# Forming the first expert block from batches 0 to 2 and routing all tokens between its products

## The chip, the cores and the metric

One Trainium2 chip, one core. The metric is the device time of one execution in microseconds (us): the median of the runs of the kernel before is 931.78 us (3 runs, 931.18 to 934.29). Engines by the names of the profile: PE is TensorE (matmuls; PEld is its weight load), DVE is VectorE, ACT is ScalarE, POOL is GpSimd (here it issues the indirect DMAs), SP is SyncE (here it issues the other DMAs).

## What is computed

Three stages in float32, one after the other on 1792 tokens (4 batches of 448) of width 768.

1. Attention, 12 heads of 64: `sigmoid(q k^T / 8 - log 448) v` for each batch. Its output is the token matrix x.
2. A mixture of 8 experts. A token takes part if `x . w_skip > 0`; it goes to the expert e with the largest of 8 logits `x @ w_gate`, and gets `x + gate * relu(x @ w1[e]) @ w2[e]`, where gate is the softmax probability of that expert (w1[e] is 768 x 1024, w2[e] 1024 x 768). Other tokens pass unchanged.
3. A dense layer pair, 768 to 2048 to 768, with an ELU between.

For the inputs of the reference (its default seed), worked out from the reference itself: 1066 tokens take part. Per expert 0 to 7 they are 0, 65, 199, 144, 391, 35, 10 and 222; of the first 1280 tokens the same counts are 0, 1, 128, 0, 298, 35, 9 and 83.

## The kernel before

Products of full precision are made of three matmuls of rounded parts: `gemm` (line 724) adds hi x hi, hi x lo and lo x hi. So each operand is split into a hi part (ACT, a copy that rounds) and a lo part (DVE, `tensor_sub`).

**Attention.** The loop at line 434 goes over n = 0 to 24. Step n computes the scores of head pair n (`scores`, line 223, PE, then a sigmoid on ACT) and the mix of pair n - 1 (`mix`, line 239, PE, then a copy to xT on DVE). Pairs 18 to 23 are batch 3. Between these the loop places, by hand, other work: the splits of the next q and k; the logits of a finished batch (`logits`, line 252, and `token_logits`, line 277); `rows(t)` (line 266), which transposes one tile of 128 tokens of xT and writes it to x_d in DRAM, for tiles 0 to 8 (`LATE = 9`); `narrow` (line 143), which converts 18 of the dense layer's weight tiles on DVE, spread evenly over the 24 pairs; and `sooner` (line 389), which picks experts for the first 10 tiles (`SOON`, 1280 tokens) and counts their places.

**Routing.** After the loop everything about the last batch is done in a row (lines 493 to 637): its logits, rows 9 to 13, the choice of experts, the counts by expert, the order of blocks, the place of each token in its block (`inv`, line 585: a product of one-hot matrices whose result is the list of tokens of every block), the gates (`ig`, line 622) and the kind of every block. PE is kept busy meanwhile with products of zeros (`keep_warm`, line 191, 28 of them) and, ahead of the first block, `hold_up` (line 739, 14 products).

**Expert blocks.** A block is up to 256 tokens of one expert, as two halves of 128. Blocks are sorted so that those with the fullest last block come first. `level(i, k)` (line 1088) handles block i: `gather` (line 696, two indirect DMAs on POOL) brings its rows of x_d into xg; `fetch` (line 684, SP) brings the expert's eight weight chunks of 768 KB into a ring of raw tiles; `split_w` (line 710) splits a chunk; `columns` (line 755) transposes xg on PE and splits it into x2; then four chunks of the product with w1 (`up_two`, line 806), and four with w2 for each half (`back`, line 857); `outcome` (line 905) adds the gated result to xg and `scatter` writes it back. Of the second product of a block three chunks of its first half are left to the next block (`between`, line 953, and `lead_in`, line 967), so that PE has work while the next x2 is split. The kind of a block, a number read into a register, decides by branches whether its second half is left out (1), takes at most 64 tokens (2) or is whole (3). In the first block 0, aside from its products, `places_in_order` (line 974) and `slot_order` (line 1029) work out an order of all tokens by expert for the dense stage.

All three of PE, ACT and DVE follow the order in which the program is written (`manual_schedule`); each engine takes its instructions strictly in that order.

Of the kernel before, what the change touches and what calls it, by code (L numbers as in the profile page):

```python
# [32 lines left out]
E = 8  # L33
# [5 lines left out]
NB = (NT + E * (BLK - 1)) // BLK  # L39
# [7 lines left out]
LATE = 9  # L47
NRAW = 13
NSPL = 4
# [5 lines left out]
SOON_STEP = (B - 1) * NP + 1  # L55
NEG = -(2**31)
# [8 lines left out]
def _constants():  # L65
# [8 lines left out]
        "row": np.arange(P)[:, None],  # L74
# [15 lines left out]
def build(nc, tc, a):  # L90
# [3 lines left out]
    with ExitStack() as top:  # L94
# [35 lines left out]
        blk_e = cp.tile([P, 1], I32, name="blk_e")  # L130

        early = top.enter_context(tc.tile_pool(name="early", bufs=1))
        raw_t = [early.tile([P, WCH], F32, name=f"raw{j}") for j in range(2)]
        wi1 = early.tile([P, DM], F32, name="wi1")
# [36 lines left out]
        ET = mybir.EngineType  # L171
        with ExitStack() as st:
            st.enter_context(tc.manual_schedule(engines={ET.PE, ET.Activation, ET.DVE}))
            xp = st.enter_context(tc.tile_pool(name="xp", bufs=1))
            rowp = st.enter_context(tc.tile_pool(name="rowp", bufs=2))
            ast = st.enter_context(ExitStack())
            qkp = ast.enter_context(tc.tile_pool(name="qkp", bufs=2))
            atp = ast.enter_context(tc.tile_pool(name="atp", bufs=2))
            cvp = ast.enter_context(tc.tile_pool(name="cvp", bufs=2))
            pss = st.enter_context(tc.tile_pool(name="pss", bufs=3, space=PSUM))  # L180
            ps1 = st.enter_context(tc.tile_pool(name="ps1", bufs=1, space=PSUM))
            psx = st.enter_context(tc.tile_pool(name="psx", bufs=1, space=PSUM))
# [18 lines left out]
            lgT = xp.tile([P, NT], F32, name="lgT")  # L201
# [50 lines left out]
            def logits(b):  # L252
                lg = psx.tile([P, 512], F32, name="lg", tag="px")
                for cc in range(KD):
# [9 lines left out]
                nc.vector.tensor_copy(lgT[:, b * S : (b + 1) * S], lg[:, :S])  # L264

            def rows(t):
                xr = rowp.tile([P, DM], F32, name="xr")
                px = pss.tile([P, 2, 512], F32, name="px", tag="ps")
                for i in range(KD):
                    g, o = i // 3, i % 3 * P  # L270
                    flip(px[:, g, o : o + P], xT[:, i, t * P : (t + 1) * P])
                nc.scalar.copy(xr.rearrange("p (g n) -> p g n", g=2), px[:, :, :N2])
# [4 lines left out]
            def token_logits(t0, n):  # L277
                pl = psx.tile([P, 4, P], F32, name="pl", tag="px")
                for i in range(n):
                    flip(pl[:, i, :], lgT[:, (t0 + i) * P : (t0 + i + 1) * P])  # L280
# [25 lines left out]
            per = [ert([1, E1], f"per{j}", BF16) for j in range(2)]  # L306
            t1 = ert([NTT, E1], "t1")
            pos_i = ert([NTT], "pos_i", I32)
            sr_i = ert([NTT, 1], "sr_i", I32)
            rt_tok = ert([NTT, P], "rt_tok", F16)  # L310

            def choices(a, z):
# [22 lines left out]
                yield  # L335
                with nc.allow_low_precision("whole numbers up to 14"):
                    nc.vector.reduce_sum(
                        per[a > 0][:, 0], oh1[:, w].rearrange("p t e -> p e t"), axis=AX.X
                    )

# [3 lines left out]
            def positions(a, z, pool, tag):  # L344

                pos = pool.tile([P, z - a, E1], F32, name="pos", tag=tag)
                n, w = z - a, oh1[:, a:z]
                if a:
                    nc.tensor.matmul(
                        pos, ones_b, per[0].to_broadcast([P, n, E1]), start=True, stop=False  # L350
                    )
                else:
                    nc.tensor.matmul(pos, zero_b[:, 0], w, start=True, stop=False)
                for o in range(1, n):
                    nc.tensor.matmul(
                        pos[:, o:, :],
                        ones_b,
                        w[:, o - 1 : o].to_broadcast([P, n - o, E1]),
                        start=False,
                        stop=False,  # L360
                        skip_group_check=True,
                    )
                nc.tensor.matmul(pos, tri_b, w, start=False, stop=True)
                return pos

            def places(a, z, pos):
# [6 lines left out]
                nc.vector.tensor_copy(pos_i[:, w], posv[:, w])  # L373
                yield
                nc.vector.tensor_scalar(sr_i[:, w, 0], pos_i[:, w], P - 1, None, op0=ALU.bitwise_and)
# [3 lines left out]

            def spots(a, z):  # L380

# [7 lines left out]
            def sooner():  # L389

                yield from choices(0, SOON)
                for _ in range(NCH):
                    yield
                pos = positions(0, SOON, psx, "px")
                yield from places(0, SOON, pos)
                yield from spots(0, SOON)
# [5 lines left out]
            def load_v(n):  # L402
                vts[n] = qkp.tile([CP, 4, NCH, D], F32, name="vt", bufs=2)
# [16 lines left out]
            zrow = rowp.tile([1, DM], F32, name="zrow", bufs=1)  # L420
            nc.gpsimd.memset(zrow, 0.0)
            nc.sync.dma_start(x_d[NT : NT + 1, :], zrow)

# [10 lines left out]
            for n in range(steps + 1):  # L434
                b, hp = divmod(n, NP)
                T, p = divmod(n, 2)
                if p == 0 and n < steps:
# [16 lines left out]
                if conv is None and narrowed < n * 2 * FA // (steps - 1):  # L454
# [898 lines left out]
```

## Time and profile before

| | |
|---|---|
| median of 3 runs | 931.78 us |
| the profiled execution's own time | 926.99 us |
| its span, first to last instruction | 925.2 us |
| mean granted TensorE clock | 0.995 |
| PE busy | 894.3 us, 97% |
| DVE busy | 556.0 us, 60% |
| ACT busy | 485.6 us, 52% |
| POOL busy | 72.3 us, 8% |
| stages | attention to 167.8 us, routing to 190.8, experts to 449.2, dense to 925.2 |

The busy time of PE counts its products of zeros too. A table of 40 slices shows PE at 8 or 9 tenths everywhere, so the places where time goes are seen only in the rows of single instructions. The profiled execution is 4.8 us shorter than the median of the runs; sums below are made against the profiled execution and carried over to the median as a difference.

### The profile page before, as it was taken

The numbers are of one execution on the slowest core, as the hardware profiler recorded it, in microseconds if no ns is written. First come the engines' busy times: TensorE is split into PE (matmuls) and PEld (weight loads), VectorE is DVE, ScalarE is ACT, GpSimd is POOL, SyncE is SP. The second block draws the span as 40 slices with busy tenths as digits, with TensorE's granted clock in tenths as the row PEclk, the third lists the DMA queues.
The fourth block names the chain that finished last, engine by engine and source line by source line (L and its number), as shares of the span: only waits on it lengthen the run. The fifth ranks groups of instructions, "written<-read, shape, count | busy, mean of one in ns | idle before, by whom it ended". The sixth has DMA issues, their size and how long they took to land.

```text
span 925.2 us, 13707 instructions
## 1 busy us (share of the span) xinstructions
PE 894.3 (97%) x5239; PEld 719.4 (78%) x5239; DVE 556.0 (60%) x862; ACT 485.6 (52%) x676; POOL 72.3 (8%) x69
## 2 busy tenths in 40 slices
PE   9999999898999998799899999999999999999998
PEld 4445555488988997688688888888888888888997
DVE  2776677766664654787588887534434533434664
ACT  7767767343454454676354554444443444443664
POOL 0000000203010310232100000100000100000100
PEclk9999999999999999999999999999999999999999
DMA  8778785599552961982653342100100100000100
GB/s 285 239 250 269 243 299 170 182 381 413 188 215 68 365 237 40 410 322 85 222 194 103 103 119 69 65 5 0 35 18 18 69 1 1 1 1 4 66 1 35
DMA packets 33909, 133.95 MB, mean 145 GB/s; under 512 B 4666, under 2 KB 5818, under 8 KB 33810
## 3 DMA queue, kind: packets, MB, share of 16 engines
q1 hardware_dynamic: 29186, 113.43, 34.7%
q0 software_dynamic: 4480, 19.01, 5.8%
q8 instruction: 57, 0.93, 0.4%
q14 instruction: 42, 0.34, 0.1%
q10 hardware_dynamic: 144, 0.23, 0.1%
HBM read 112.08 MB, written 23.60 MB: 147 GB/s over the span
## 4 chain that ended last, share of the span: by engine, by line
PE 94%; DVE 2%; issue 1%; ACT 1%; DMA 1%; POOL 0%; ACTq 0%; DVEq 0%; POOLq 0%
PE acc L1228 16%; PE pt L1228 10%; PE acc L1195 8%; PE acc L1196 8%; PE acc L1197 8%; PE po L242 8%; PE ps L228 7%; PE acc L725 6%; PE acc L726 6%; PE acc L727 6%; PE pt L138 1%; PE acc L797 1%; PE acc L138 1%; PE acc L798 1%; PE px L138 1%
## 5 line engine op out<-in xcount | busy, mean ns | idle before, releaser
L718 DVE TENSOR_TENSOR wlo<-raw,whi 128x1536 fp32r<-128x1536 f32 x64 | 111.3, 1755 | 36.6 <-ACT whi L716 32.6
L1204 ACT ACTIVATE m<-acc 128x512 f32<-128x512 f32 (+1 forms) x64 | 34.9, 545 | 174.0 <-PE acc L1197 167.1
L1206 DVE SCALAR_TENSOR_TENSOR m<-m,acc 128x512 f32<-128x512 f32 (+1 forms) x64 | 39.7, 620 | 137.6 <-ACT m L1205 137.6
L716 ACT CAST whi<-raw 128x1536 fp32r<-128x1536 f32 x64 | 94.0, 1481 | 29.9 <-PE acc L727 9.0
L235 ACT ACTIVATE at<-ps,bias 112x896 f32<-112x896 f32 x96 | 88.9, 1009 | 28.3 <-PE ps L228 27.9
L1228 PE MATMUL acc<-wol,gh 128*128 128x256 f32 x320 | 101.0, 316 | 0.0
L1228 PE MATMUL acc<-woh,gl 128*128 128x256 f32 x320 | 100.5, 314 | 0.0
L1228 PE MATMUL acc<-woh,gh 128*128 128x256 f32 x320 | 100.4, 314 | 0.0
L1196 PE MATMUL acc<-x,wih 128*128 128x512 f32 (+1 forms) x270 | 96.0, 356 | 0.0
L1195 PE MATMUL acc<-x,wih 128*128 128x512 f32 (+1 forms) x270 | 95.9, 355 | 0.0
L1197 PE MATMUL acc<-x,wil 128*128 128x512 f32 (+1 forms) x270 | 95.6, 354 | 0.0
L725 PE MATMUL acc<-whi,both 128*128 128x384 f32 (+1 forms) x236 | 84.4, 357 | 3.4 <-issue 3.4
L726 PE MATMUL acc<-wlo,both 128*128 128x384 f32 (+1 forms) x236 | 83.1, 352 | 0.0
L727 PE MATMUL acc<-whi,both 128*128 128x384 f32 (+1 forms) x236 | 83.1, 352 | 0.0
L242 PE MATMUL po<-at,vt 112*64 112x448 f32 x384 | 77.5, 545 | 0.7 <-DVE xT L250 0.7
L1184 DVE TENSOR_TENSOR wol<-wo,woh 128x768 fp32r<-128x768 f32 x64 | 61.2, 956 | 23.4 <-ACT woh L1183 23.0
L1228 PEld LDWEIGHTS acc<-woh,gh 128*128 128x128 f32 x320 | 60.3, 188 | 10.1
L1228 PEld LDWEIGHTS acc<-wol,gh 128*128 128x128 f32 x320 | 60.3, 188 | 9.3
L1183 ACT CAST woh<-wo 128x768 fp32r<-128x768 f32 x64 | 53.4, 834 | 26.0 <-PE acc L1228 25.9
L1210 DVE TENSOR_TENSOR gl<-m,gh 128x512 fp32r<-128x512 f32 (+1 forms) x64 | 40.0, 625 | 40.5 <-ACT gh L1209 40.5
L1178 DVE TENSOR_TENSOR wil<-wi,wih 128x768 fp32r<-128x768 f32 x60 | 57.4, 956 | 11.0 <-ACT wih L1177 6.0
L1228 PEld LDWEIGHTS acc<-woh,gl 128*128 128x128 f32 x320 | 60.1, 188 | 4.3
(235 smaller groups left out, 1881.5 us busy)
## 6 DMA issues: line engine op xcount, KB each, us to landing
raw<-in_w SPq DMA_DIRECT2D x66, 768.0 KB
raw<-in_wi SPq DMA_DIRECT2D x9, 768.0 KB
raw<-in_wo SPq DMA_DIRECT2D x9, 768.0 KB
vt<-in_v SPq DMA_DIRECT2D x12, 448.0 KB
x_d<-xr SPq DMA_DIRECT2D x14, 384.0 KB
raw<-in_wi SPq DMA_DIRECT2D x14, 384.0 KB
raw<-in_wo SPq DMA_DIRECT2D x14, 384.0 KB
qr<-in_q SPq DMA_DIRECT2D x11, 448.0 KB
```

The costliest lines, as they stand in the source:

```text
L228: nc.tensor.matmul(ps[:CP, j, :S], kk[head, p, c * CP : (c + 1) * CP], qq[head, p], start=(i == 0), stop=(i == 2),)
L235: nc.scalar.activation(at[:, :, c, :], ps[:CP, :, :S], AF.Sigmoid, bias=bias[:CP], scale=QK_SCALE)
L242: nc.tensor.matmul(po[64 * j : 64 * j + 64, :S], vt[:, 2 * (hp % 2) + j, c, :], at[:, j, c, :], start=(c == 0), stop=(c == NCH - 1),)
L716: nc.scalar.copy(w_hi, raw)
L718: nc.vector.tensor_sub(w_lo, raw, w_hi)
L725: nc.tensor.matmul(o, a_hi, b_hi, start=first, stop=False)
L726: nc.tensor.matmul(o, a_hi, b_lo, start=False, stop=False)
L727: nc.tensor.matmul(o, a_lo, b_hi, start=False, stop=last)
L1195: nc.tensor.matmul(o, a, b, start=(cc == 0), stop=False)
L1196: nc.tensor.matmul(o, a, c, start=False, stop=False)
L1197: nc.tensor.matmul(o, wil[:, cc], b, start=False, stop=(cc == KD - 1))
L1228: nc.tensor.matmul(o, a, b, start=(clears and f == 0 and k_ == 0), stop=(f == KF2 - 1 and k_ == 2), skip_group_check=True,)
```

## The change

1. **A first block from 1280 tokens.** `sooner` starts one step earlier. It now takes the expert with the most tokens among batches 0 to 2, takes its first 256 tokens (`took`), and with ten small products (`inv0`) makes the list of their rows, `slot_0`, in step 23. `gather_first` brings them into xg. Its weights are fetched by the expert's number `blk_0`: chunks 0 and 1 at step 23, 2 and 3 at step 24 into tiles that lie where q and k lay, 4 and 5 behind them, 6 and 7 once the raw tiles of 0 and 1 are split.
2. **The first products follow the attention.** `columns(0)` comes right after the last mix. `first_block` computes the block without branches; its 256 places are all computed.
3. **The routing goes between its products.** `routing()` is a generator with a step behind each of the 16 groups of nine products with w1, and four behind each chunk with w2: the last batch's token logits, rows 10 to 13, counts (less `took`), places, lists, gates, kinds, then `places_in_order`. All `keep_warm` calls behind the attention and `hold_up` are gone. The remaining tokens make blocks 1 and up (`NB` is one larger, `RING`-tile lgT, slots count from block 1).
4. **What moves into the attention.** `rows(9)` (`LATE = 10`; rows 7 to 9 at steps 19 to 21), the 18 conversions (now done by step 21 instead of 23, and all of them written to DRAM, so that wi1 is read back), the first four of six products of the last batch's logits (ahead of the last mix).
5. **Pools.** The x2 tile, xT and the attention's tiles move to the other side of SBUF, so that the weight tiles can take q's and k's place early; `rows_of` in the dense stage reuses two xg tiles.

How the instructions move, at the three places that the prediction speaks of. First PE, from the end of the attention on. Before (po is the mix, lg the logits, px rows, pl the token logits):

```order
L242 MATMUL po<-at,vt 64x448 x16
L256 MATMUL lg<-xT,wgs 32x448 x6
L138 MATMUL px<-cst,xT 128x128 x6
L138 MATMUL pl<-cst,lgT 128x128 x4
L138 MATMUL px<-cst,xT 128x128 x12
```

And in the change, from the last of the ten products of inv0 (pc are the first transposes of the gathered rows; twelve of them follow, then two more logit products of L271, then the first expert product, L548):

```order
L479 MATMUL inv_1797<-a_192,rt_tok 128x2
L256 MATMUL po<-at,vt 64x448 x8
L271 MATMUL lg<-xT,wgs 32x448 x4
L256 MATMUL po<-at,vt 64x448 x8
L142 MATMUL pc<-cst,xg_108 128x128
L142 MATMUL pc<-cst,xg_109 128x128
```

The last two mixes are now parted by four logit products, and twelve transposes of gathered rows and the other two logit products are all that stands between the last mix and the first expert product. Second DVE, inside the first block: the choice of experts for the last batch ends, then two splits of weights stand among the routing's instructions.

```order
L373 TENSOR_TENSOR oh<-sc,m_175 128x4x8
L541 TENSOR_TENSOR wlo_1835<-raw_107,whi_1834 128x1536
L745 SCALAR_TENSOR_TENSOR ni<-acc_1908,took 128x8
L748 TENSOR_SCALAR nb<-ni 128x8
L751 TENSOR_SCALAR last<-ni 128x8
L752 SCALAR_TENSOR_TENSOR rank<-last,early_cst 128x8
L756 TENSOR_TENSOR first<-rank 128x64
L759 TENSOR_TENSOR tmp<-nb,first 128x64
L760 TENSOR_REDUCE span<-tmp 128x8
L541 TENSOR_TENSOR wlo_1913<-raw_1836,whi_1912 128x1536
```

Before, the routing's instructions stood ahead of all splits but that of chunk 0; now the splits of chunks 1 to 7 and the copies of the block stand between them. Third POOL: the two gathers of the first block (xg_108 and xg_109, by slot_0) come ahead of the last batch's choice of experts (oh 128x4), which before came ahead of every gather.

```order
L524 DMA xg_108<-x_d,slot_102 128x768
L524 DMA xg_109<-x_d,slot_102 128x768
L356 TENSOR_SCALAR oh<-lgt 128x4
L771 TENSOR_TENSOR posk<-posv,skip 128x4
L513 DMA xg_1918<-x_d,slot_tok 128x768
L513 DMA xg_1919<-x_d,slot_tok 128x768
```

The gathers of block 1 (xg_1918 and xg_1919) wait for the lists of all blocks, slot_tok.

The core of the diff:

```diff
-LATE = 9
+LATE = 10
+NRAW0 = 6
...
             def sooner():
 
...
+                bank = psx.tile([P, 512], F32, name="pos", tag="px")
+                pos, count = positions(0, SOON, bank)
+                yield
+                nc.vector.scalar_tensor_tensor(
+                    key, count, float(E), con("ramp")[:, :E], op0=ALU.mult, op1=ALU.add
+                )
+                yield
+                nc.vector.reduce_max(kmax, key, axis=AX.X)
...
+                nc.vector.scalar_tensor_tensor(
+                    took[:, 0], count, float(BLK), sel, op0=ALU.min, op1=ALU.mult
+                )
...
+                yield from wait(SOON_STEP + 4, 0)
+                inv = psx.tile([P, 512], F32, name="inv0", tag="px")[:, :2]
+                for t in range(SOON):
+                    nc.tensor.matmul(
+                        inv, rt_tok[:, t, :], a0[:, t, :], start=(t == 0), stop=(t == SOON - 1)
+                    )
+                yield
+                nc.vector.tensor_scalar_add(slot_0, inv, float(NT))
+                gather_first()
...
+                if n == steps - 1:
+                    assert narrowed == 2 * FA
+                    fetch(0, range(2))
+                if n == steps:
+                    qst.close()
...
+                    some_weights(tokp, 2, 2)
+                    fetch(0, range(2, 4))
+                    lg = logits(B - 1, None, range(KD - 2))
...
-                if conv is None and narrowed < n * 2 * FA // (steps - 1):
+                if conv is None and narrowed < min(2 * FA, n * 2 * FA // (steps - 3)):
...
             run(soon)
-            logits(B - 1)
+            columns(0, [pss.tile([P, 2, 512], F32, name="pc", tag="ps")[:, 0] for _ in range(3)])
+            logits(B - 1, lg, range(KD - 2, KD))
...
+            def routing():
...
+                token_logits(done_lgt, NTT - done_lgt, acc_t[5])
+                yield
+                choose(SOON, NTT)
+                split_w(0, 1, hi=False)
+                fetch(0, range(NRAW0, 8))
+                rows(LATE, banks)
+                yield
+                rows(LATE + 1, banks)
+                pos, cnt = positions(SOON, NTT, acc_t[5])
...
+                inv = acc_t[4][:, :NHB]
+                for t in range(NTT):
+                    nc.tensor.matmul(
+                        inv, rt_tok[:, t, :], aa[:, t, :], start=(t == 0), stop=(t == NTT - 1)
+                    )
+                nc.vector.tensor_scalar_add(slot_tok, inv, float(NT))
+                gather(1, False)
...
+                coming = kind(1)
...
+                fetch(1, range(2))
+                yield from places_in_order()
+                yield
+                order_rows()
...
+            def first_block(aside):
+
+                for c in range(4):
+                    nh, c3 = divmod(c, 2)
+                    for f in range(4):
+                        up_one(0, c, f)
+                        next(aside, None)
+                        if c3:
+                            h_one(4 * nh + f)
+                        if f == 2:
+                            ahead(0, c)
+                ahead(0, 4)
+                for c in range(4, 8):
+                    if c == 5:
+                        ahead(0, 5)
+                    back(0, 1, P, range(c, c + 1))
+                    for _ in range(4):
+                        next(aside, None)
+                outcome(0, 1, P)
+                run(aside)
+                back(0, 0, P, range(4, 5))
+                slot_order()
...
-            fetch(0, range(1))
-            first_rows = gather(0, False)
-            issued = nc.gpsimd.memset(slot_off[:, NHB:], 0.0)
-            tc.add_manual_dep(issued.ins, first_rows[1].ins.name, AFTER)
-            fetch(0, range(1, 2), [issued])
-            fetch(0, range(2, 8), first_rows)
-            gather(1, False)
-            split_w(0, 0)
-            level(0, kind(0))
+            first_block(routing())
+            level(1, coming)
```

`up_one` and `h_one` are the bodies of the loop of `up_two`: nine products of 256 columns, and the ReLU copy to h2 with its lo part.

## Rows read from the trace of the kernel before

**Rows 1.** The chain of work that ended last: shares of the span by engine.

```profile
PE 94%; DVE 2%; issue 1%; ACT 1%; DMA 1%; POOL 0%; ACTq 0%; DVEq 0%; POOLq 0%
```

**Rows 2.** Windows: length, busy us (count) of PE, PEld, DVE, ACT, POOL, clock, DMA.

```profile
0.00:157.77 157.77, 155.67 (x1030) 77.63 (x1030) 104.52 (x163) 114.72 (x130) 2.07 (x11) 1.00 0.77 255
...
167.80:190.75 22.95, 18.54 (x142) 10.80 (x142) 14.46 (x58) 8.51 (x12) 5.72 (x6) 1.00 0.73 255
190.75:218.70 27.95, 27.95 (x216) 27.79 (x217) 20.29 (x43) 12.78 (x15) 0.00 (x0) 1.00 1.00 402
```

**Rows 3.** Timeline of PE, last mixes and routing (start, length, instruction, [idle before]).

```profile
160.61 3.23 PE L242 MATMUL po<-at,vt 112*64 112x448 f32 x16
164.57 3.23 PE L242 MATMUL po<-at,vt 112*64 112x448 f32 x16 [0.73 <-DVE xT L250]
167.72 1.74 PE L256 MATMUL lg<-xT,wgs 128*32 128x448 f32 x12
169.39 0.88 PE L138 MATMUL px<-cst,xT 128*128 128x128 f32 x6
170.18 0.66 PE L138 MATMUL pl<-cst,lgT 128*128 128x128 f32 x4
...
177.04 1.08 PE L585 MATMUL inv<-aa,rt_tok 128*128 128x28 f16 x14 [1.35 <-ACT ex L596]
...
181.12 0.52 PE L622 MATMUL ig<-av,rt_tok 128*128 128x56 f16 x14 [0.26 <-DVE av L610]
...
187.45 0.99 PE L138 MATMUL pt<-cst,xg 128*128 128x128 f32 x7 [0.30 <-DMA xg<-x_d,slot_tok]
```

**Rows 4.** Groups by line (busy, mean ns): zero products of 167 to 219; all weight splits.

```profile
L195 PE MATMUL idle<-zero_b 128*128 128x512 bf16 x28 | 6.5, 378 | 0.0
...
L718 DVE TENSOR_TENSOR wlo<-raw,whi 128x1536 fp32r<-128x1536 f32 x64 | 111.3, 1755 | 36.6 <-ACT whi L716 32.6 <-issue 2.3 <-DMA raw<-in_w 1.7
```

**Rows 5.** Timeline of DVE: list of slots, first splits of x2, a weight split.

```profile
178.16 0.18 DVE L589 TENSOR_SCALAR slot_tok<-inv 128x28 int32<-128x28 f32 x1 [0.28 <-PE inv L585]
...
188.66 1.29 DVE L753 TENSOR_TENSOR both<-pt,both 128x512 fp32r<-128x512 f32 x2 [3.98 <-ACT both L751]
...
223.83 1.76 DVE L718 TENSOR_TENSOR wlo<-raw,whi 128x1536 fp32r<-128x1536 f32 x1 [0.57 <-ACT whi L716]
```

**Rows 6.** POOL's gathers: timeline, and the landing time of tile xg, 170 to 262.

```profile
223.24 0.94 POOL L699 DMA_INDIRECT xg<-x_d,slot_ext  x1 [0.30 <-issue]
224.49 1.92 POOL L699 DMA_INDIRECT xg<-x_d,slot_ext  x1 [0.30 <-issue]
...
DMA to landing us min/median/max: 6.7/7.6/9.7
```

**Rows 7.** Timeline of PE: start of block 1, products behind its gap, a later gap.

```profile
218.70 0.64 PE L138 MATMUL pt<-cst,xg 128*128 128x128 f32 x4
220.61 0.65 PE L138 MATMUL pt<-cst,xg 128*128 128x128 f32 x4 [1.28 <-DVE order L1047]
...
229.85 0.18 PE L1084 MATMUL acc<-iota_h 128*128 128x2 f16 x1 [1.85 <-issue]
...
233.26 0.41 PE L726 MATMUL acc<-both,whi 128*128 128x256 f32 x1
233.48 0.41 PE L727 MATMUL acc<-both,wlo 128*128 128x256 f32 x1
...
234.41 0.28 PE L727 MATMUL acc<-both,wlo 128*128 128x256 f32 x1
234.53 0.28 PE L725 MATMUL acc<-both,whi 128*128 128x256 f32 x1
...
375.52 0.44 PE L725 MATMUL acc<-whi,both 128*128 128x384 f32 x1 [3.40 <-issue]
```

**Rows 8.** Windows behind those two gaps of PE (the columns of Rows 2).

```profile
232.00:234.00 2.00, 2.00 (x11) 2.00 (x11) 2.00 (x3) 0.96 (x1) 0.00 (x0) 0.51 0.99 402
...
376.00:378.00 2.00, 2.00 (x13) 1.96 (x12) 0.19 (x2) 0.02 (x1) 1.44 (x2) 1.00 1.01 421
```

More of the change, by code (lines that the diff above doesn't have):

```diff
@@ L389, in sooner, with wait @@
             def sooner():
+                def wait(*when):
+                    while now < when:
+                        yield
                 yield from choices(0, SOON)
-                for _ in range(NCH):
-                    yield
-                pos = positions(0, SOON, psx, "px")
-                yield from places(0, SOON, pos)
-                yield from spots(0, SOON)
+                yield from wait(SOON_STEP + 2, 0)
+                w, sh = slice(0, SOON), [P, SOON, E]
+                bank = psx.tile([P, 512], F32, name="pos", tag="px")
@@ new lines, in fetch, with gather @@
+            def fetch(i, chunks):
+                if i == NB:
+                    return
+                e = nc.values_load(
+                    blk_e[i : i + 1, :1] if i else blk_0[:1],
+                    engines=[mybir.EngineType.SP], min_val=0, max_val=E - 1,
+                )
+                for c in chunks:
+                    src = (w1, w2)[c // 4][bass.ds(e, 1), c % 4].rearrange("o p f -> (o p) f")
+                    nc.sync.dma_start(raw_of(i, c), src)
+            def gather(i, late=True):
+                at = slot_ext if late else slot_tok
+                for h in range(2):
+                    nc.gpsimd.indirect_dma_start(
+                        out=xg_t[i % NXG][h][:],
+                        out_offset=None,
+                        in_=x_d[:, :],
+                        in_offset=bass.IndirectOffsetOnAxis(
+                            ap=at[:, 2 * i + h : 2 * i + h + 1], axis=0
+                        ),
+                    )
@@ L635, in build @@
[L635 to L646 removed]
+            pst.close()
@@ L755, in columns @@
-            def columns(i):
-                for g in range(3):
-                    flip_rows(i, g, ends[g])
-                    split_columns(g, ends[g], x2)
+                        inv, rt_tok[:, t, :], aa[:, t, :], start=(t == 0), stop=(t == NTT - 1)
+                    )
+                nc.vector.tensor_scalar_add(slot_tok, inv, float(NT))
+                gather(1, False)
+                nc.vector.tensor_scalar(taken, inv, 0.0, None, op0=ALU.is_lt)
+                nc.vector.tensor_copy(slot_off[:, :NHB], inv)
@@ new lines, in routing @@
+                yield
+                ig = acc_t[5][:, : 2 * NHB].rearrange("p (s n) -> p s n", s=2)
+                for t in range(NTT):
+                    nc.tensor.matmul(
+                        ig, rt_tok[:, t, :], av[:, t], start=(t == 0), stop=(t == NTT - 1)
+                    )
+                nc.vector.tensor_add(
+                    kinds,
+                    kn.rearrange("p (b h) -> p b h", h=2)[:, :, 1],
+                    taken[:1].rearrange("p (b h) -> p b h", h=2)[:, :, 0],
+                )
```

678 lines of the change are left out of this document (343 added, 335 removed).

## The prediction

> **What bounds the kernel now.** I read the chain that ended last first. It is 94% PE [rows 1], so only two things shorten the kernel: taking work from PE, or filling time in which PE waits or does nothing useful. Next come the windows by stage [rows 2]. In the attention PE is busy 155.67 of 157.77 us; nothing is to be had there, and VectorE (104.52 us) has room. In block 0 PE is busy 27.95 of 27.95 us. Between them lies the routing, 167.80 to 190.75: 22.95 us without a single expert product. PE is shown busy there for 18.54 us, but 6.5 us are products of zeros [rows 4], 14 more zero products are those of `hold_up`, and most of the rest is small: six logit products 1.67 us, one `rows` 0.8 us (five of them), token logits 0.5, `inv` 1.1, `ig` 0.5 [rows 3]. The change can only win out of these 22.95 us.
>
> **What stays.** The number of blocks. There are 64 weight splits, eight to a block, so 8 blocks run before [rows 4]. Of the first 1280 tokens expert 4 has 298, the most; the first block takes 256, which leaves it 391 - 256 = 135. With 222, 199, 144, 65, 35 and 10 of the others that is seven more blocks: 8 again, with the same mixture of whole and small ones. So the sum needs only the time at which block 1's `columns` begin on PE: before, 218.70 [rows 7].
>
> **The sum, step by step.**
>
> (a) PE's end of the attention. The mix of pair 23 ended at 164.57 + 3.23 = 167.80 [rows 3]. Ahead of it now stand `rows(9)`, +0.8 (169.39 to 170.18), the ten products of `inv0`, +0.8 (10 of 14 parts of the 1.08 of `inv`), and four of six logit products, 4/6 of 1.67 = 1.1, of which 0.7 fills the wait for the xT copy ahead of the last mix [rows 3], so +0.4. That makes 169.8. The 18 conversions are only moved to earlier steps; VectorE's third of idle time in the attention covers them. If it does not in some step, PE waits there for a score's operands; I take 0 and keep up to 2 us in the range.
>
> (b) The gather. `inv0` follows the scores of step 23, where the mix at 160.61 stood; with `rows(9)` it runs from 161.4 to 162.2. The list `slot_0` is a VectorE instruction like `slot_tok`, 0.28 behind its product [rows 5]: 162.5. For block 0 it took 187.45 - 178.16 = 9.3 us from that instruction to the first rows' use on PE [rows 3, 5], with weights loading beside it as now. So the rows are there at 171.8, and PE, free at 169.8, waits 2.0. Landing times ran from 6.7 to 9.7 [rows 6]; 187.45 was at the short end, so the bounds are 171.8 and 174.8, or 169.8 if the gather finds the queues emptier.
>
> [...]
>
> (c) Transposes and first splits of x2. From the first transpose to the end of the second lo split it took 188.66 + 1.29 - 187.45 = 2.5 us [rows 3, 5], and the first products need no more than these. They begin at 174.3. The remaining two logit products hide behind the splits.
>
> (d) The block's own work: 27.95 [rows 2].
>
> (e) The routing's work on PE, now between products: `rows` 10 to 13, 4 x 0.8; token logits 0.5; positions 0.5 (taken like `ig`); `inv` 1.1; `ig` 0.5 [rows 3]. Together 5.8.
>
> (f) New waits inside the block. VectorE has to do 20.29 us of block 0 and, of the 14.46 us of the routing [rows 2], all but the split of chunk 0 (1.8), the x2 splits (2.0) and an xT copy (0.6): 10.1. That is 30.4 us beside PE's 27.95 + 5.8 = 33.75. In total it fits, but VectorE takes its work in order: a token's place that PE waits for can stand behind a weight split of 1.755 us [rows 4], and a ReLU part behind the routing. The lower bound is 0 (block 0 ran without a gap), the upper all of the 10.1. Laying the three queues beside each other by these durations I find four waits: 0.8 for an accumulator that a late ReLU copy frees, 0.4 for `ig`'s operand, 0.9 for the kind of block 1 being read into registers (between nothing, as in the gapless row, and the 1.85 in front of a branch [rows 7]; I take the middle), and 1.1 for the lo parts of chunks 5 to 7, which come late because the routing went first. I take 3.2: it is nearest to the gapless row, since VectorE has a tenth to spare.
>
> Sum: 174.3 + 27.95 + 5.8 + 3.2 = 211.25 instead of 218.70, which is 7.45 us earlier. From block 1 on the program is the same; its 1.28 us wait for `order` and its 1.85 us gap, with products 0.21 us apart behind it instead of 0.12 [rows 7], are assumed to stay. The profiled execution took 926.99 us, so 919.5; it lies 4.8 under the median of the runs, and the same difference from 931.78 gives **924.3**.
>
> **Where the POOL queue could hurt.** Beside a VectorE split at 223.83 a gather took 1.92 us to issue instead of 0.94 [rows 5, 6]: 1.0 us. The first gathers are issued some 1 to 2.5 us behind `slot_0`, at 163 to 165; the split of chunk 0 stands behind the last xT copy, near 167, and does not meet them, so 0 in the sum and +1.0 in the range. [...]
>
> **The rivals.**
>
> R1, the gather is in time: no wait of 2.0, 922.3. For it: the last scores leave POOL and the queues empty. Against: landings of 6.7 to 9.7 [rows 6]. Chance 0.12.
>
> R2, the gap at the start of block 1 goes too. The 1.85 us of "issue" came as PE arrived at a branch [rows 7]; behind it the clock was 0.51 [rows 8]. From 230.10 to 234 some 18 products ran at 0.2145 instead of 0.1178, 1.75 us lost. If the kind is known long before, both vanish: 3.6 less, 920.7. For it: the kind is now read in the middle of the block. Against: a like gap of 3.40 stands ahead of 375.52 [rows 7], 190 us after the kinds were worked out. Chance 0.15.
>
> R3, VectorE sets the pace of the block. If its 10.1 us of routing lie fully on the path, (f) is 10.1 instead of 3.2: 931.2, no change that can be measured. For it: VectorE is nine tenths full and in order. Against: in total it fits. Chance 0.15.
>
> R4, slower: the clock. The zero products kept PE running through the routing; now nothing does while PE waits for the rows, and inside the block short waits follow each other. [...] For it: 0.51 behind a gap of 1.85. Against: 1.00 behind a gap of 3.40 [rows 8]; one fall that lasts as long as at 230 costs 1.75, which is in my range. Chance 0.06.
>
> R5, the change does not do what it says: the first block is not full, and a ninth block follows. Even one that leaves out its second half costs half of a whole block's 27.95 [rows 2], 14 us: 938. The counts speak against it. Chance 0.02.
>
> **How the numbers follow.** Forecast 0.50, R1 0.12, R2 0.15, R3 0.15, R4 0.06, R5 0.02. A measurement of this kernel tells 0.3%, 2.8 us, from no change; faster means under 929.0, slower over 934.6. Faster: the forecast but 0.03 of it, R1, R2, and 0.02 of R3, 0.76. The same: most of R3 and the rest of the forecast, 0.15. Slower: R4, R5 and 0.01 of R3, 0.09. The range reaches down to R1 and R2 together with a little less waiting, 918.5 (924.3 - 2.0 - 3.6 = 918.7), and up to R3, 931.0, which also takes in the forecast with a landing 3 us later, a fall of the clock (1.75) and 1.0 on POOL.
>
> **What would show it.** Right: PE's last mix ends near 169.8, a wait of about 2 us for the gathered rows, the first product near 174.3, block 1's transposes near 211, no zero products behind the attention, the same 64 weight splits. (b) is wrong if the wait is none or over 4 us; (f) if the waits inside the block sum to under 1 or over 6 us, and R3 holds if nearly all of them end with VectorE; R4 shows as a granted clock near 0.5 for over 20 us. The prediction falls if a wait appears in the attention itself, from the conversions done earlier, or if a transfer other than the gather (a weight chunk fetched into q's and k's place) is what the first products wait for.

## The result

The changed kernel takes 920.18 us (median of 4 runs, 918.73 to 922.78), the kernel before 931.48 (4 runs, 930.91 to 934.29). The ratio is 0.9876, 95% interval 0.9846 to 0.9906. That is 11.3 us, or 1.2%, less. Forecast were 924.3 us and a range of 918.5 to 931.0.

The profiled execution of the changed kernel took 919.79 us (span 918.0), close to its median. That of the kernel before took 926.99 and lay 4.5 under the median of 931.48, so the two profiles show only 7.2 us of the 11.3. A second profile of the kernel before, taken in the experiments, lies at its median (931.06, span 929.3). The table puts all three beside each other; times are starts on PE, in us from the start of the span. Starts in different profiles are not quite alike: the first product of the attention starts at 7.09 in the second profile and 7.11 in the changed kernel, but at 6.46 in the first, and from 5.73 to 8.38 over all the profiles below.

| | before, first profile | before, second profile | changed |
|---|---|---|---|
| first expert product | 190.75 | 191.35 | 177.69 |
| transposes of block 1 | 218.70 | 219.31 | 214.75 |
| transposes of block 2 | 259.27 | 261.00 | 249.85 |
| end of the span | 925.2 | 929.3 | 918.0 |
| block 1, length | 40.57 | 41.69 | 35.10 |
| from block 2 to the end | 665.9 | 668.3 | 668.2 |

Against the second profile the difference is 4.56 us up to block 1's start, 6.59 in block 1 and 0.15 in all the rest. The forecast had 7.45 in the first part and nothing in the second. Each column is a single profile, and the last row of the two of the kernel before differs by 2.4 us, so differences of a microsecond or two over the whole span mean little.

The timeline of PE after the change (columns as in [rows 3]); all waits between the attention and block 1 are in it:

```profile
161.89 0.40 PE L479 MATMUL inv<-a,rt_tok 128*128 128x2 f16 x10
162.22 3.23 PE L256 MATMUL po<-at,vt 112*64 112x448 f32 x16
...
166.26 3.23 PE L256 MATMUL po<-at,vt 112*64 112x448 f32 x16
170.62 0.33 PE L142 MATMUL pc<-cst,xg 128*128 128x128 f32 x1 [1.13 <-DMA xg<-x_d,slot]
173.87 2.61 PE L142 MATMUL pc<-cst,xg 128*128 128x128 f32 x11 [2.91 <-DMA xg<-x_d,slot]
176.40 1.36 PE L271 MATMUL lg<-xT,wgs 128*32 128x448 f32 x4
177.69 0.39 PE L548 MATMUL acc<-both,whi 128*128 128x256 f32 x1
...
192.65 0.86 PE L801 MATMUL acc<-aa,rt_tok 128*128 128x30 f16 x4 [0.55 <-DVE rt_tok L422]
...
196.20 0.39 PE L548 MATMUL pt<-both,whi 128*128 128x256 f32 x1 [1.54 <-DVE both L932]
...
201.95 0.36 PE L548 MATMUL pt<-both,whi 128*128 128x256 f32 x1 [0.61 <-DVE kinds L835]
...
210.34 0.44 PE L549 MATMUL acc<-wlo,both 128*128 128x384 f32 x1 [0.30 <-DVE wlo L541]
...
214.75 1.07 PE L142 MATMUL pt<-cst,xg 128*128 128x128 f32 x8
...
225.61 0.28 PE L549 MATMUL acc<-both,whi 128*128 128x256 f32 x1 [0.47 <-issue]
```

The 0.73 us in front of the last mix [rows 3] are gone, and nothing in block 1 answers to the 1.28 and 1.85 us of [rows 7]; 0.47 us of `issue` is left at 225.61, some 3 us behind the branch. The windows (columns as in [rows 2]) of the wait for the rows, the transposes, the block and the place where the kernel before had its gap:

```profile
169.49:173.87 4.38, 0.33 (x3) 0.14 (x2) 0.62 (x1) 0.00 (x0) 0.00 (x0) 1.00 1.01 396
173.87:177.69 3.82, 3.82 (x15) 2.39 (x15) 1.95 (x3) 1.76 (x3) 0.00 (x0) 0.55 0.58 236
177.69:214.75 37.06, 33.89 (x286) 32.01 (x285) 30.21 (x95) 15.70 (x24) 3.02 (x4) 1.00 0.57 204
...
222.00:226.00 4.00, 3.53 (x30) 3.28 (x30) 1.87 (x2) 2.85 (x2) 3.39 (x3) 1.00 1.03 399
```

While PE waits, the DMA engines are full (share 1.01, 396 GB/s). The transposes then run at a granted clock of 0.55. In the block VectorE is busy 30.21 of 37.06 us (forecast 30.4), and the clock is 1.00. The list of rows (`slot_0`, on DVE), the gathers on POOL and their landing time (as [rows 6]):

```profile
162.33 0.16 DVE L483 TENSOR_SCALAR slot<-inv 128x2 int32<-128x2 f32 x1 [0.52 <-PE inv L479]
...
163.38 1.23 POOL L524 DMA_INDIRECT xg<-x_d,slot  x1 [6.04 <-DMA raw<-in_w]
164.92 1.00 POOL L524 DMA_INDIRECT xg<-x_d,slot  x1 [0.31 <-issue]
...
DMA to landing us min/median/max: 7.2/8.0/8.9
```

Both are issued in 1.0 to 1.2 us, where the one beside a split of VectorE had taken 1.92 [rows 6], and VectorE's next split starts at 166.03, behind both; so no split held them up, they are late in landing. From the second issue to the use of its rows it is 173.87 - 164.92 = 8.95 us, where the kernel before had 6.76 (issued at 180.69, used at 187.45 [rows 3]); its DMA share over that time was 0.87, here it is 1.01. The chain that ended last is less of PE than in [rows 1], with the two waits for the gather and VectorE's in it:

```profile
PE 91%; DVE 3%; ACT 2%; issue 2%; DMA 1%; POOL 0%; DVEq 0%; ACTq 0%; POOLq 0%
```

### The profile page after: what moved, and what is told of

Its sections match the earlier page's. It is cut to its first block, busy times and chain, and to the rows that moved or that the text cites. A ratio compares the mean times of both kernels' runs of the same rounds, so it can differ in the third digit from the quotient of the medians.

```text
span 918.0 us, 13615 instructions
## 1 busy us (share of the span) xinstructions
PE 887.1 (97%) x5208; PEld 714.6 (78%) x5208; DVE 557.7 (61%) x872; ACT 485.3 (53%) x679; POOL 75.6 (8%) x76
## 4 chain that ended last, share of the span: by engine, by line
PE 91%; DVE 3%; ACT 2%; issue 2%; DMA 1%; POOL 0%; DVEq 0%; ACTq 0%; POOLq 0%
PE acc L1331 16%; PE pt L1331 10%; PE acc L1298 8%; PE acc L1299 8%; PE acc L1300 8%; PE po L256 8%; PE ps L242 7%; PE acc L549 5%; PE acc L548 5%; PE acc L550 5%; PE acc L142 1%; PE acc L907 1%; PE acc L908 1%; DVE wlo L541 1%; PE pt L142 1%
## 5 line engine op out<-in xcount | busy, mean ns | idle before, releaser
L541 DVE TENSOR_TENSOR wlo<-raw,whi 128x1536 fp32r<-128x1536 f32 x64 | 111.3, 1756 | 31.8 <-ACT whi L539 31.2
L548 PE MATMUL acc<-whi,both 128*128 128x384 f32 (+1 forms) x236 | 84.8, 359 | 0.0
```

Of the source, the lines that this page charges most:

```text
L541: nc.vector.tensor_sub(w_lo, raw, w_hi)
L548: nc.tensor.matmul(o, a_hi, b_hi, start=first, stop=False)
```

## The experiments

Two questions stood. Why was block 1's start, at 214.75, 3.5 us later than the 211.25 of the forecast? And why did block 1 itself lose 6.6 us, where nothing in it was changed?

### The wait for the gathered rows

**Chunks 4 and 5 behind the gather.**

```diff
-            fetch(0, range(4, NRAW0))
+            fetch(0, range(4, NRAW0), first_rows)
```

(`fetch` makes each transfer wait for those named last, as the kernel before did.)

> Only chunks 4 and 5 of the first block's weights wait until both gathers have landed. Theory A (the first gather lands late, 8.95 us behind its issue, because weight chunks keep the DMA queues full; 396 GB/s and a DMA share of 1.01 at 169.5 to 173.9): chunks 2 and 3 still stand ahead, chunk 4 no longer, so the second half lands near 171, PE waits 1 to 2 us instead of 4.04 and the first expert product starts 2 to 3.5 us earlier than 177.69. Rival A' (the landing time is the gather's own latency, whatever else is loading): second half at 173.9 +- 0.5, no change.

Measured: 919.56 us, ratio to before 0.9878 (0.9843 to 0.9912). PE:

```profile
170.91 2.51 PE L142 MATMUL pc<-cst,xg 128*128 128x128 f32 x11 [1.78 <-DMA xg<-x_d,slot]
```

Its second gather was issued at 163.59, so its rows are used 7.3 us later instead of 8.95. PE waits 0.65 + 1.78 = 2.4 instead of 4.04, and the first product starts at 174.76. The way is that of theory A, but this run alone does not show it: the other profiles of the changed kernel whose loads were left alone and whose PE waits for the rows (four experiments below and the one with 70 products at the start) have 7.59 to 8.74 us from issue to use and 2.68 to 3.84 us of waiting, so 7.3 and 2.4 lie only just outside. Of the 2.9 us by which the first product is earlier, 1.3 lie in the attention, which ended earlier. The median moved less than the runs scatter.

**Chunks 2 to 5 behind the gather.**

```diff
-                    fetch(0, range(2, 4))
...
-            fetch(0, range(4, NRAW0))
+            fetch(0, range(2, NRAW0), first_rows)
```

> Chunks 2 to 5 wait until both gathers have landed. Theory A: the gather finds nearly empty queues and lands near 169.5 to 170.5, PE waits under 1 us, the transposes run at the full clock (2.5 us instead of 3.82) and the first expert product starts near 173, 4 to 5 us earlier; about 915.5 us. Price to watch: chunks 2 and 3 then land 4 to 6 us later than now, and their splits could be late (chunk 2's hi part is made at 183.4). Rival A': landing near 173.9, no gain, or a loss from late chunks.

Measured: 919.77 us, ratio 0.9875 (0.9842 to 0.9908). First PE, then SP (its transfers):

```profile
170.16 1.42 PE L142 MATMUL pc<-cst,xg 128*128 128x128 f32 x11 [1.64 <-DMA xg<-x_d,slot]
...
172.39 0.39 PE L555 MATMUL acc<-both,whi 128*128 128x256 f32 x1
...
186.65 1.54 PE L142 MATMUL acc<-cst,xT 128*128 128x128 f32 x6 [5.71 <-ACT xr L296]
```

```profile
170.32 7.98 SPq L513 DMA_DIRECT2D raw<-in_w  x6
178.35 10.69 SPq L297 DMA_DIRECT2D x_d<-xr  x4
```

The first half: rows used 6.5 us behind their issue (163.69), which is outside the 7.6 to 8.95 of the kernels whose loads were left alone, with a DMA share of 0.40 over that time instead of 1.01; the transposes run at the full clock (granted 1.00), and the first product starts at 172.39, 5.3 us earlier than in the changed kernel, of which 1.2 lie in the attention. The second half: all of it was given back. Six chunks now stand on SP ahead of the writes of rows 10 to 13; the write at 178.35 took 7.7 us to land (median in the changed kernel 2.4), ScalarE's copy of a row tile waits 6.20 us for it, and PE waits 5.71 us for ScalarE. The chunks that were put behind the gathers came ahead of these writes instead.

**All loads put in order, and one split moved.** The third edit is the next experiment's.

```diff
-                    fetch(0, range(2, 4))
...
-            fetch(0, range(4, NRAW0))
+            fetch(0, range(2, 4), first_rows)
...
-                split_w(0, 1, hi=False)
-                fetch(0, range(NRAW0, 8))
...
                 rows(LATE + 3, banks)
+                fetch(0, range(4, 8), row_writes[-1:], AFTER)
...
+            split_w(0, 1, hi=False)
             columns(0, [pss.tile([P, 2, 512], F32, name="pc", tag="ps")[:, 0] for _ in range(3)])
```

> Three edits together: chunks 2 and 3 wait for the gathers, chunks 4 to 7 are issued behind the last write of rows 10 to 13, and the lo split of chunk 1 stands ahead of the block. By theory A the first product is near 172.5 as in the run with chunks 2 to 5 behind the gather; by the queue theory of that run's 5.71 us wait (SP issued six chunks ahead of the writes of rows, and the ScalarE copy of row tile 12 waited for a write) that wait is gone, so that the waits inside the block sum to under 2 us. Block 1's transposes then start near 207 instead of 214.75, the time is 910 to 914 us. Rival: the waits come back in another place (chunk 2 or 4 late), start of block 1 not before 210.

Measured: 912.26 us (910.04 to 915.27), ratio 0.9826 (0.9778 to 0.9873): by the medians 18.6 us under the kernel before in the same runs, by the ratio some 16. It is 8 us under the changed kernel by medians of separate runs, which do not overlap (that kernel's fastest is 918.73), while the intervals of the two ratios still do. PE:

```profile
170.12 1.42 PE L142 MATMUL pc<-cst,xg 128*128 128x128 f32 x11 [1.03 <-DMA xg<-x_d,slot]
...
172.34 0.39 PE L560 MATMUL acc<-both,whi 128*128 128x256 f32 x1
...
188.76 0.39 PE L560 MATMUL pt<-both,whi 128*128 128x256 f32 x1 [0.39 <-DVE both L943]
...
194.58 0.36 PE L560 MATMUL pt<-both,whi 128*128 128x256 f32 x1 [0.67 <-DVE kinds L846]
...
202.96 0.44 PE L561 MATMUL acc<-wlo,both 128*128 128x384 f32 x1 [0.30 <-DVE wlo L553]
...
207.38 1.07 PE L142 MATMUL pt<-cst,xg 128*128 128x128 f32 x8
```

The wait of 5.71 is gone, the waits in the block sum to 1.36, and block 1 starts at 207.38, where it was expected. The rows are used 170.12 - 164.25 = 5.9 us behind their issue. Both theories hold together: the loads delayed the gather (8.95 us beside them, 5.9 here), and their order on SP decided whether PE paid for it elsewhere (5.71 us with six chunks ahead of the writes, nothing here).

### VectorE inside the block

```diff
-                split_w(0, 1, hi=False)
...
+            split_w(0, 1, hi=False)
             columns(0, [pss.tile([P, 2, 512], F32, name="pc", tag="ps")[:, 0] for _ in range(3)])
```

> The lo split of weight chunk 1 (1.755 us of VectorE) is moved from between the routing's steps to the time in which VectorE waits for the gathered rows. Theory C (the waits of PE inside the block, 0.55 for rt_tok, 1.54 for the lo part of h, 0.61 for the kinds, 0.30 for a lo split, come from VectorE being full from 179 to 214 and taking its work in order): the sum of these waits falls from 3.0 to about 1.3, block 1's transposes start 1.5 us earlier than 214.75. Rival C' (each wait has its own chain of small instructions that no spare time on VectorE ahead of it shortens): sum 2.7 to 3.3.

Measured: 917.89 us, ratio 0.9857 (0.9821 to 0.9893). The waits left in the block, on PE:

```profile
193.35 0.38 PE L548 MATMUL pt<-both,whi 128*128 128x256 f32 x1 [0.42 <-DVE both L932]
...
199.10 0.36 PE L548 MATMUL pt<-both,whi 128*128 128x256 f32 x1 [0.61 <-DVE kinds L835]
...
207.48 0.44 PE L549 MATMUL acc<-wlo,both 128*128 128x384 f32 x1 [0.30 <-DVE wlo L541]
```

They sum to 1.33 instead of 3.00, as theory C said: one split of 1.755 us, moved to where VectorE stands idle, took 1.67 us of waiting from PE. The wait of 1.54 for the lo part of h shows it best: it is 1.53 to 1.56 in the five other profiles, above and below, that leave the split in its place and have no long wait ahead of it, 0.42 here and 0.39 with all loads in order.

### The clock behind the wait

```diff
+            keep_warm(19)
             columns(0, [pss.tile([P, 2, 512], F32, name="pc", tag="ps")[:, 0] for _ in range(3)])
```

> 19 products of zeros (4 us) stand between the last mix and the first transpose, nothing else changes. Theory B (the transposes and the first splits take 3.82 us instead of 2.5 because PE stood still 4.04 us and the clock was granted 0.55 there): the clock stays at 1.00, the first product is 1.0 to 1.5 us earlier, at 176.4. Rival B' (what is slow are the ACT and DVE splits of x2 in their chain behind the transposes): no change within 0.3 us.

Measured: 924.77 us, ratio 0.993 (0.9899 to 0.996), 4.6 us slower than the changed kernel. PE:

```profile
172.76 1.77 PE L142 MATMUL pc<-cst,xg 128*128 128x128 f32 x12
174.46 0.95 PE L271 MATMUL lg<-xT,wgs 128*32 128x448 f32 x4
176.25 0.39 PE L548 MATMUL acc<-both,whi 128*128 128x256 f32 x1 [0.85 <-DVE both L565]
...
224.06 0.16 PE L1196 MATMUL acc<-iota_h 128*128 128x2 f16 x1 [3.12 <-issue]
```

The slow products are gone: the two logit products take 0.95 instead of 1.36 us, as in the run with chunks 2 to 5 held back, where the granted clock was 1.00. But a wait of 0.85 us for the splits stands where the slow products were, so from the transposes to the first product it is 3.49 instead of 3.82, not 2.5; the run with 70 products at the start has the same 0.85 without zero products in the wait; why it is missing in the run with chunks 2 to 5 held back (2.23 in all) stays open. The loss is elsewhere: a gap of 3.12 us in block 1, which is 40.7 us long again.

### The gap in block 1

The second profile of the kernel before:

> The kernel before, unchanged, for a second profile. If its 1.28 us wait for order and its 1.85 us issue gap at block 1 belong to the program, they stand in it again within 0.3 us each, and block 1 takes 40.6 +- 0.5 us; if the gap is chance, it is gone or over 1 us different.

Its PE, start of block 1 to start of block 2 (as [rows 7]):

```profile
219.31 0.63 PE L138 MATMUL pt<-cst,xg 128*128 128x128 f32 x4
221.22 0.66 PE L138 MATMUL pt<-cst,xg 128*128 128x128 f32 x4 [1.28 <-DVE order L1047]
...
231.56 0.18 PE L1084 MATMUL acc<-iota_h 128*128 128x2 f16 x1 [2.95 <-issue]
261.00 1.03 PE L138 MATMUL pt<-cst,xg 128*128 128x128 f32 x8
```

The 1.28 belong to the program. The gap is there again, but 2.95 instead of 1.85. Its cause was tried from three sides. First, **the kind read late**:

```diff
-                coming = kind(1)
...
             first_block(routing())
+            coming = kind(1)
             level(1, coming)
```

> The kind of block 1 is read into registers behind the first block instead of inside it. By the reason that the prediction gave for its rival on the gap (a kind that is known early lets PE pass the branch of block 1 without a gap): the wait of 0.61 us in the block goes and a gap of 2 to 4 us comes back at the branch, block 1 later by 1.5 to 3 us. Against it (the gap is not about when the kind is known): 0.6 us less in the block, up to 1 us more ahead of block 1, no other gap, no change of the time within 1 us.

Measured: 919.05 us, ratio 0.9875 (0.983 to 0.992). No gap comes back at the branch; block 1 takes 251.79 - 216.48 = 35.3 us. So the gap does not hang on how early the kind is known. That block 1 started 1.7 us later in that profile has another reason, the clock: it was 0.50 over the transposes, and behind the wait for the lo part of h, as long as in the changed kernel, it fell once more, to 0.50, while there it was 1.00 from 196.20 to 203.00 (PE, then the window behind it):

```profile
195.80 0.58 PE L548 MATMUL pt<-both,whi 128*128 128x256 f32 x1 [1.56 <-DVE both L931]
```

```profile
197.00:199.00 2.00, 2.00 (x12) 2.00 (x11) 1.93 (x4) 0.00 (x0) 1.70 (x2) 0.50 0.37 81
```

Second, **19 products of zeros, 16 columns wide, at the very start** of the changed kernel:

```diff
             keep_warm(15)
+            tiny = pss.tile([P, 4, P], F32, name="tiny", tag="ps")
+            for _ in range(19):
+                nc.tensor.matmul(
+                    tiny[:, 0, :16], zero_b[:, 0], zero_b[:, 0, :16], start=True, stop=True
+                )
```

> 19 zero products of 16 columns at the very start, nothing else: as many PE instructions more as in the run with zero products in the wait, but 160 us earlier. That run had a gap of 3.12 us (issue) at block 1's first branch and 40.7 us for block 1 instead of 35.1. Theory D (the gap hangs on where PE's instructions lie, so that the same shift brings it back wherever it is made): gap of 2 to 4 us at the branch of block 1, block 1 about 40 us, about 924 us. Rival D' (it hangs on what happened in time around the wait for the rows): no gap, block 1 35.1 us, the time up by no more than 1.5 us for the tiny products themselves.

Measured: 925.26 us (10 runs), ratio 0.9947 (0.9926 to 0.9967). The products cost 0.6 us at 6.5; PE 210 us later:

```profile
216.25 1.07 PE L142 MATMUL pt<-cst,xg 128*128 128x128 f32 x8
...
226.85 0.16 PE L1200 MATMUL acc<-iota_h 128*128 128x2 f16 x1 [2.85 <-issue]
256.13 1.03 PE L142 MATMUL pt<-cst,xg 128*128 128x128 f32 x8
```

The gap is back, and block 1 takes 39.9 us. Third, the same at the start of the kernel before, 19 and 70 of them, and 70 in the changed kernel:

> The kernel before with 19 zero products of 16 columns at the start. Theory D (where PE's instructions lie decides on the gap at block 1's first branch): a shift can take the gap of 1.85 to 2.95 us away as it brought it into the changed kernel; then block 1 takes about 37 us instead of 40.6 to 41.7 and the time is 926 to 928 us; or it stays, which alone decides nothing. Rival D'' (the gap belongs to block 0 standing in a branch of its own in the kernel before): gap of 1.8 to 3 us under every shift.

> The same with 70 such products, some 2 us more of PE at most. Theory D: the gap of block 1 differs between the shifts of 0, 19 and 70, and is under 1 us for at least one. Rival D'': 1.8 to 3 us here too.

> The changed kernel with 70 such products at the start. Theory D: block 1 is at one of its two values, 35.1 us without and about 40 us with the gap; the wait of 1.28 us for order does not come back. That the gap comes only with a shift of 19 would be seen here as 35.1.

Measured against the unchanged kernel before (929.79, 27 runs): before with 19, 931.87 us, ratio 1.0028 (0.9997 to 1.0058), gap 2.78 and block 1 41.1 us long; before with 70, **923.38 us**, ratio 0.9934 (0.9916 to 0.9952), no gap; changed with 70, 920.67 us, ratio 0.9913 (0.988 to 0.9946), no gap. PE of the kernel before with 19, with 70, and of the changed kernel with 70 (wait for the rows, start of block 1, start of block 2):

```profile
232.44 0.19 PE L1089 MATMUL acc<-iota_h 128*128 128x2 f16 x1 [2.78 <-issue]
```

```profile
221.25 0.64 PE L138 MATMUL pt<-cst,xg 128*128 128x128 f32 x4
223.17 0.66 PE L138 MATMUL pt<-cst,xg 128*128 128x128 f32 x4 [1.28 <-DVE order L1052]
...
258.07 1.04 PE L138 MATMUL pt<-cst,xg 128*128 128x128 f32 x8
```

```profile
173.26 1.42 PE L142 MATMUL pc<-cst,xg 128*128 128x128 f32 x11 [1.83 <-DMA xg<-x_d,slot]
...
214.68 0.53 PE L142 MATMUL pt<-cst,xg 128*128 128x128 f32 x3
...
249.14 1.03 PE L142 MATMUL pt<-cst,xg 128*128 128x128 f32 x8
```

In the kernel before with 70, block 1 takes 36.82 us, with the wait of 1.28 and without the gap. That kernel became 6.4 us faster by 70 products that compute nothing. Rival D'' falls: the gap does not belong to block 0 standing in a branch. It comes and goes with the number of products that PE has ahead of it: with 0, 19 and 70 more it is 1.85 or 2.95, 2.78 and none in the kernel before, none, 2.85 and none in the changed one. That it hangs on the time at which PE arrives instead does not fit: seven of the profiled kernels here have the same 5208 products on PE (the changed one, the four with loads or a split moved, the late kind and the one of the next section), their block 1 starts anywhere from 207.38 to 223.08, and none has more than 0.51 us of `issue` in it. The gap stands at a branch; what PE waits for there is not shown by any run.

### Overlap or not

```diff
-            first_block(routing())
+            aside = routing()
+            run(aside)
+            first_block(aside)
```

> The changed kernel with the whole routing ahead of the first product of the first block instead of between its products; the first rows are still gathered early. If the gain at block 1's start comes from the overlap: the routing's 15 us (167.8 to 183 before) stand alone again, the first product moves from 177.7 to about 190, the block takes 28 to 29 us, block 1's transposes start near 218 to 219 instead of 214.75, and the gain there against the kernel before is gone. Rival (the gain is the zero products and the wait for the block's own list that fell away): block 1 starts within 1 us of 214.75.

Measured: 930.55 us, ratio 0.9997 (0.9975 to 1.0019): no faster than the kernel before. PE:

```profile
188.42 0.17 PE L795 MATMUL acc<-per,ones_b 128*128 128x9 bf16 x1 [5.29 <-ACT xr L296]
...
193.79 0.56 PE L548 MATMUL acc<-both,whi 128*128 128x256 f32 x1
...
223.08 1.07 PE L142 MATMUL pt<-cst,xg 128*128 128x128 f32 x8
```

With the routing ahead, block 1 starts 8.3 us later than in the changed kernel (expected were 3.3 to 4.3). The excess is about PE's wait of 5.29 us for ScalarE, which waits 5.36 for a write of rows; that a weight chunk issued at 181.36, ahead of that write, delays it is likely from the run with chunks 2 to 5, but was not tried here. To leave this wait out is an estimate: counted from the attention's first product, block 1 then starts at 223.08 - 5.29 - 6.41 = 211.4, against 207.6 in the changed kernel and 212.2 in the second profile before. So of the 4.6 us gained at block 1's start some 3.7 come from the overlap; the rival, that it is all the zero products and the wait for the list, falls.

## Why the prediction was right, and where not

The time lay in the range and the sign was right, but two errors partly cancelled: up to block 1 the gain was 4.56 us instead of 7.45 (by the start itself 214.75 instead of 211.25), and in block 1, where nothing was forecast, it was 6.59. That the time comes within 0.6 us of R2's 920.7 is luck in the same way: R2 has the 7.45 in full and only 3.6 of the 6.59.

**Step (a) held.** The last mix ended at 166.26 + 3.23 = 169.49; forecast was 169.8. The attention's earlier conversions cost nothing: ahead of the gather no new wait stands on PE. `inv0` took 0.33 instead of 0.8.

**Step (b) failed**, at "with weights loading beside it as now". The list came at 162.33, as forecast (162.5), but the second half of the rows was used at 173.87, not at 171.8: 11.54 us from the list to their use, where 9.3 were carried over from the kernel before. PE waited 1.13 + 2.91 = 4.04 us instead of 2.0, just over the 4 us that the prediction had named as a sign that (b) is wrong. Weights did load beside the gather in the kernel before, but fewer (DMA share 0.87 from the second issue to the use, 1.01 in the changed kernel): the gathers of block 0 did not share the DMA engines with chunks 2 to 7, which waited for them (`first_rows` in the diff), and the change takes that wait away. The experiments show the price of what stood beside the gather: 8.95 us from issue to use as it is (7.59 to 8.95 over six profiles with these loads), 7.3 without chunks 4 and 5, 6.5 and 5.9 without chunks 2 to 5. R1, the gather in time, did not happen.

**Step (c)** was mis-sized: 3.82 us instead of 2.5, at a clock of 0.55 behind the wait. With the clock at 1.00 the same stretch took 2.2 us in the two runs with chunks 2 to 5 held back, and 3.1 and 3.5 in two where the logit products were as short as there (0.94 and 0.95 us) but PE waited 0.85 for a split. The fall of the clock stood in the range, not in the sum.

**Steps (d) to (f) held.** From the first product to block 1 it took 37.06 us; forecast was 27.95 + 5.8 + 3.2 = 36.95. The waits sum to 0.55 + 1.54 + 0.61 + 0.30 = 3.00 (3.2), if not by the parts that were named: the ReLU part of h cost 1.54 (0.8), the kinds 0.61 (0.9), the lo parts 0.30 (1.1), `ig` nothing (0.4), and `rt_tok` 0.55 was not foreseen. That VectorE's order makes them is shown by the split that was moved (3.00 us of waits to 1.33). R3 needs care: its sign was that nearly all waits in the block end with VectorE, and all four do. But its price was 10.1 us of waiting, and they sum to 3.00, so the block did not run at VectorE's pace; the sign was too weak to tell R3 from the forecast.

**"Assumed to stay" failed.** Neither the 1.28 nor the 1.85 us of [rows 7] is in the changed kernel, and behind the branch the clock is 1.00 (222 to 226), where behind the gap it was 0.51 [rows 8]. R2 had named the gap and priced it at 3.6, with a chance of 0.15, but for a reason that the run with the late kind refutes. The gap goes with the number of PE's instructions ahead of it, so it is luck that the changed kernel has none: with 19 products more it has one. Of the 6.59 us the gap and the slow products behind it are 41.69 - 36.82 = 4.9, by the kernel before with 70 products (granted clock 0.62 from the gap's end at 231.56 to 236 in the second profile, 1.00 from 231 to 236 with 70); 1.28 is the wait, and some 0.4 is left. Why the 1.28 goes is not shown: block 0 no longer stands in a branch, and all four profiles of the kernel before, shifted or not, have it, and none of the changed kernel's. It is not that `order` comes sooner: VectorE makes it 1.7 us after the transposes start in both (220.39 - 218.70 before, 216.45 - 214.75 after).

So not all of the 11.3 us are the overlap's. Compared with the gap in both, the changed kernel with 19 products stands 0.53% under the kernel before, some 5 us. Compared without it in either, with 70 products in both, it is 920.67 against 923.38, 2.7 us; but there the kernel before has lost a second gap as well, that of 3.40 us in block 5 [rows 7], and has one of 1.94 ahead of block 3, while the changed kernel has one of 3.67. At block 1's start, which these gaps do not touch, the three pairs of profiles (no products, 19, 70), counted from the attention's first product, give 4.6, 3.5 and 6.0 us. The forecast's 7.45 lies above all of these.

R4 and R5 did not happen: no stretch of 20 us at the lower clock (the longest, behind a gap of 3.71 us, starts at 366.48 and ends before 372: 0.50 from 365 to 370, 1.00 from 372), and 64 weight splits (L541, x64) as before.

## What to carry to other kernels

A row's duration is worth only what stood beside it (here 6.76 us from a gather's issue to its use at a DMA share of 0.87, 8.95 at 1.01): before a latency is taken over, look at which other transfers the old program held back and the new one lets go. Six chunks put behind the gathers delayed the writes of rows that followed them on SP (7.7 us to land instead of 2.4, 5.71 us of waiting on PE), so set the order of a whole queue at once, not one wait at a time. Where a kernel branches, shift it by a few dozen idle instructions before crediting a change with a few microseconds: here 70 of them alone were worth 6.4 us (929.79 to 923.38).

## What the runs showed of the hardware that was not expected

- Products that compute nothing, 210 us ahead, switched a gap of PE at a branch on or off: none, 2.85 and none with 0, 19 and 70 of them in the changed kernel; 1.85 or 2.95, 2.78 and none in the kernel before.
- Equal waits of PE were not always followed by the lower clock. Behind 1.54 us the granted clock stayed at 1.00 in the changed kernel, and behind 1.56 us in the same place it fell to 0.50 with the kind read late. Behind the gather's wait the eleven transposes took 2.61 us after a wait of 1.82 (19 products at the start) and 1.42 after one of 1.83 (70 products). What decides it is not shown.
- A gather of 2 x 393,216 bytes took 7.59 to 8.95 us from the second issue to its use beside weight chunks 2 to 5 (DMA share 1.01 in the changed kernel), and 5.9 to 6.5 us without them (0.40 to 0.47).
